# One fixed order for the first loads of an attention-plus-MLP kernel, with V as fp32 through SP's queue

## The chip, the cores and the metric

The kernel runs on one core of a Trainium2 chip. The metric is device time in microseconds (us), the median of the fast executions. A profile's span, from the first to the last instruction of the profiled execution, is about 2 us shorter than the time.

Engines in the profile: PE is the matmul engine (PEld its weight load), DVE the vector engine, ACT the scalar engine, POOL the engine called gpsimd in code, SP the engine that issues most loads. "SPq" is SP issuing.

## The reference

Eight batches, eight heads, 576 positions, head size 64. A sliding-window attention with a linear bias is followed by a normalised MLP with a residual:

```
scores = where(0 <= i - j < 128, q @ k.T / 8 - slope[h] * (i - j), -1e9)
x      = softmax(scores) @ v                    # -> (8, 576, 512)
xn     = (x - mean(x)) / sqrt(var(x) + 1e-6) * g
out    = x + relu(xn @ w1) @ w2                 # w1 512 x 2048, w2 2048 x 512
```

All inputs are fp32. The kernel computes in fp16 with fp32 accumulation.

## The kernel before

Attention works on head pairs: four per batch, `hp` 0 to 3. Each needs a q, a k and a V tile. The MLP works on chunks of 512 rows, nine in all, and is interleaved with the attention of the next batch. Batch 0's attention has no MLP to hide behind, and the first MLP chunk needs the first 512 of batch 0's 576 rows and all of w1. So everything up to the first MLP matmul is a head in which PE is mostly idle.

```python
def load_qk(b, hp):                      # fp32, issued by SP: six DMAs per head pair
    i = (b * HPAIRS + hp) % NSTG
    for src, dst in ((q, q32[i]), (k, k32[i])):
        ...
def load_v_all(b):                       # converted to fp16 on the way, issued by POOL
    ...
load_qk(0, 0)
nc.sync.dma_start(out=iden, ...)         # needed by every transpose
nc.sync.dma_start(out=mband, ...)        # masks, 512 KB
load_qk(0, 1)
nc.sync.dma_start(out=g_sb, ...)
load_v_all(0)
# ... cut: the mask copies on POOL, then
load_qk(0, 2)
load_qk(0, 3)
load_weights()                           # POOL: w1 in 4 column quarters, then w2 in 4
load_v_all(1)
scale_w1()                               # DVE: w1 *= g, 16 pieces of 128x512
drive(attn_gen(0), None, 0.0)
for c in range(NCHUNK):
    drive(attn_gen(c + 1) if c + 1 < B else None, mlp_gen(c), 1.0)
```

In `attn_gen` each head pair casts q and k to fp16 (DVE), transposes them on PE, copies the transposes out (`dst`), makes scores (`sc`), exponentials (ACT) and mask multiplies (`probs`, DVE), and multiplies by V (`ppv`). When a batch is done, DVE normalises it (`xs`), PE transposes it (`pxt`) and ACT copies it out (`xt`). `pm` is an MLP matmul. A scheduler decides the order on each engine ahead of time. At run time each engine works in that order, as the traces show it: in the changed kernel a statistics step of DVE (`mv`) had its input at 44.5 us and ran at 55.3, behind a cast for whose load DVE stood 10.2 us.

The softmax here doesn't subtract the row's maximum and nothing guards it: scores larger than these inputs give would overflow.

Of the kernel before, what the change touches and what calls it, by code (L numbers as in the profile page):

```python
# [10 lines left out]
FP32 = mybir.dt.float32  # L11
# [5 lines left out]
def kernel(  # L17
# [64 lines left out]
    NSTG = 4  # L82
    q32 = [persist.tile([P, NSB, 2, D], FP32, tag=f"q32{i}", name=f"q32_{i}") for i in range(NSTG)]
    k32 = [persist.tile([P, NSB, 2, D], FP32, tag=f"k32{i}", name=f"k32_{i}") for i in range(NSTG)]
    for t in q32 + k32:
        nc.vector.memset(t[TAIL:P, NSB - 1, :, :], 0.0)

    def load_qk(b, hp):
        i = (b * HPAIRS + hp) % NSTG
        for src, dst in ((q, q32[i]), (k, k32[i])):  # L90
            s = src[b, 2 * hp : 2 * hp + 2, :, :]
            for g in range(2):
                nc.sync.dma_start(  # L93
                    out=dst[:, 0:NFULL, g, :],
                    in_=s[g, 0 : NFULL * P, :].rearrange("(sb p) d -> p sb d", p=P),
                )
            nc.sync.dma_start(  # L97
                out=dst[0:TAIL, NFULL, :, :],
                in_=s[:, NFULL * P : S, :].rearrange("h p d -> p h d"),
            )  # L100

    vext = [persist.tile([P, NSB, H, VD], FP16, tag=f"vx{i}", name=f"vx_{i}") for i in range(2)]

    def load_v(b, hp):
        dst = vext[b % 2]
        s = v[b, 2 * hp : 2 * hp + 2, :, :]
        for sb in range(NSB):
            pb = P if sb < NFULL else TAIL
            nc.gpsimd.dma_start(
                out=dst[0:pb, sb, 2 * hp : 2 * hp + 2, 0:D],  # L110
                in_=s[:, sb * P : sb * P + pb, :].rearrange("h p d -> p h d"),
            )

    def load_v_all(b):
        dst = vext[b % 2]
        for sb in range(NSB):
            pb = P if sb < NFULL else TAIL
            nc.gpsimd.dma_start(  # L118
                out=dst[0:pb, sb, :, 0:D],
                in_=v[b, :, sb * P : sb * P + pb, :].rearrange("h p d -> p h d"),  # L120
            )

    nc.scalar.preload_act_table_set("natural_log_exp_and_others")
    eps_t = consts.tile([P, 1], FP32)
    nc.vector.memset(eps_t, eps)
    load_qk(0, 0)
    iden = consts.tile([P, P], FP16)
    nc.sync.dma_start(out=iden, in_=iden_dram.ap())
    mband = consts.tile([P, H, 2 * P], FP16)
    nc.sync.dma_start(out=mband, in_=m_dram.ap())  # L130
    load_qk(0, 1)
    g_sb = consts.tile([P, NKB], FP32)
    nc.sync.dma_start(out=g_sb, in_=moe_g_ln.rearrange("(kb p) -> p kb", p=P))
    for t in vext:
        nc.vector.memset(t[:, :, :, D:VD], 1.0)
        nc.vector.memset(t[TAIL:P, NSB - 1, :, :], 0.0)
    load_v_all(0)
    m2g = consts.tile([P, H, 512], FP16)
    nc.gpsimd.tensor_copy(m2g[:, :, 0:192], mband[:, :, 0:192])
    nc.gpsimd.tensor_copy(m2g[:, :, 192:256], mband[:, :, 0:64])  # L140
    nc.gpsimd.tensor_copy(m2g[:, :, 256:512], mband[:, :, :])
    xs_tail = [persist.tile([P, d_model], FP16, tag=f"xst{i}", name=f"xst_{i}") for i in range(2)]
    for t in xs_tail:
        nc.vector.memset(t[TAIL:P, :], 0.0)
# [3 lines left out]
    w1r = moe_w_ch1.rearrange("(kb p) f -> p kb f", p=P)  # L148
    w2r = moe_w_ch2.rearrange("(fb p) d -> p fb d", p=P)

    def load_weights():
        for f0 in range(0, ffn, 512):
            nc.gpsimd.dma_start(out=w1sb[:, :, f0 : f0 + 512], in_=w1r[:, :, f0 : f0 + 512])
        for f0 in range(0, NFB, 4):
            nc.gpsimd.dma_start(out=w2sb[:, f0 : f0 + 4, :], in_=w2r[:, f0 : f0 + 4, :])

    def scale_w1():
        for f0 in range(0, ffn, 512):
            for kb in range(NKB):
                nc.vector.tensor_scalar(  # L160
                    out=w1sb[:, kb, f0 : f0 + 512],
                    in0=w1sb[:, kb, f0 : f0 + 512],
                    scalar1=g_sb[:, kb : kb + 1],
                    scalar2=None,
                    op0=ALU.mult,
                )
# [10 lines left out]
    def attn_gen(b):  # L177
# [7 lines left out]
        for hp in range(HPAIRS):  # L185
            i = (b * HPAIRS + hp) % NSTG
            tr = []
            for stg, nm in ((q32[i], "q"), (k32[i], "k")):
                s16 = st16_pool.tile([P, NSB, P], FP16, tag=f"{nm}16")
                nc.vector.tensor_copy(  # L190
                    out=s16[:, :, :], in_=stg[:, :, :, :].rearrange("p s h d -> p s (h d)")
                )
                ptr = att_psum.tile([P, NSB * P], FP16, tag="att")
                for sb in range(NSB):
                    nc.tensor.transpose(  # L195
                        ptr[:, sb * P : sb * P + P], s16[:, sb, :], iden[:, :]
                    )
                dst = qt_pool.tile([P, NSB * P], FP16, tag=f"{nm}t")
                nc.vector.tensor_copy(out=dst[:, :], in_=ptr[:, :])  # L199
                tr.append(dst)  # L200
                yield
            nxt = b * HPAIRS + hp + NSTG
            if nxt < B * HPAIRS:
                load_qk(nxt // HPAIRS, nxt % HPAIRS)
            qt, kt = tr
            pr = []
            for grp in range(2):
                sc = sc_psum.tile([P, 2, 512], FP32, tag="sc")
                for j in ORDER[grp]:
                    for g in range(2):  # L210
                        r0 = D * g
                        nc.tensor.matmul(  # L212
                            sc[:, g, OFF[j] : OFF[j] + NQ[j]],
                            kt[r0 : r0 + D, j * P : j * P + P],
                            qt[r0 : r0 + D, j * P : j * P + NQ[j]],
                            start=True,
                            stop=True,
                        )
                probs = probs_pool.tile([P, 2, 512], FP16, tag=f"pr{grp}")
                nc.scalar.activation(  # L220
                    out=probs[:, :, :], in_=sc[:, :, :], func=AF.Exp, scale=inv_sqrt_d
                )
                if grp == 0:
                    view = probs[:, :, :].rearrange("p g (t c) -> p g t c", t=2)
                    nc.vector.tensor_tensor(  # L225
                        out=view,
                        in0=view,
                        in1=mband[:, 2 * hp : 2 * hp + 2, :]
                        .unsqueeze(2)
                        .broadcast_to([P, 2, 2, 2 * P]),  # L230
                        op=ALU.mult,
                    )
                else:
                    nc.vector.tensor_tensor(  # L234
                        out=probs[:, :, :],
                        in0=probs[:, :, :],
                        in1=m2g[:, 2 * hp : 2 * hp + 2, :],
                        op=ALU.mult,
                    )
                pr.append(probs)  # L240
                yield
            for g in range(2):
                h = 2 * hp + g
                ppv = att_psum.tile([P, NSB, D + 1], FP32, tag="att")
                for qb in range(NSB):
                    nc.tensor.matmul(  # L246
                        ppv[:, qb, :],
                        pr[GRP[qb]][:, g, OFF[qb] : OFF[qb] + P],
                        vx[:, qb, h, 0 : D + 1],
                        start=True,  # L250
                        stop=(qb == 0),
                    )
                    if qb > 0:
                        j = qb - 1
                        nc.tensor.matmul(  # L255
                            ppv[:, qb, :],
                            pr[GRP[j]][:, g, OFF[j] + P : OFF[j] + 2 * P],
                            vx[:, j, h, 0 : D + 1],
                            start=False,
                            stop=True,  # L260
                        )
                rec = small_pool.tile([P, NSB], FP32, tag="rec")
                nc.vector.reciprocal(out=rec[:, :], in_=ppv[:, :, D])  # L263
                nc.vector.tensor_tensor(
                    out=xb[:, 0:NSB, D * h : D * h + D],
                    in0=ppv[:, :, 0:D],
                    in1=rec[:, :].unsqueeze(2).broadcast_to([P, NSB, D]),
                    op=ALU.mult,
                )
                yield  # L270
        if b + 2 < B:
            load_v_all(b + 2)
        if b % 2 == 1:
            xp = xpair[b // 2]
            nc.sync.dma_start(
# [104 lines left out]
                if next(m_gen, StopIteration) is StopIteration:  # L380
                    m_gen = None

    load_qk(0, 2)
    load_qk(0, 3)
    load_weights()
    load_v_all(1)
    scale_w1()
    drive(attn_gen(0), None, 0.0)
    for c in range(NCHUNK):
        drive(attn_gen(c + 1) if c + 1 < B else None, mlp_gen(c), 1.0)  # L390

# [29 lines left out]
```

## Time and profile before

402.95 us (402.53 to 403.23 in three runs).

| stretch of the trace | length |
|---|---|
| start to first MLP matmul (head) | 75.8 us |
| first MLP matmul to the end | 324.8 us |
| start of MLP chunk 1 | 114.3 us |

Busy time by stretch of the kernel before: a window and its length in us, then the busy us (and count) of each engine, the granted clock, the share of DMA time and GB/s.

```profile
core 0: us, PE busy (x) PEld busy (x) DVE busy (x) ACT busy (x) POOL busy (x), PEclk, DMA share, GB/s
0.00:76.00 76.00, 18.59 (x178) 13.18 (x179) 32.08 (x93) 12.74 (x18) 22.70 (x30) 1.00 1.20 172
200.00:300.00 100.00, 99.26 (x787) 48.66 (x788) 70.81 (x169) 46.32 (x74) 8.40 (x10) 1.00 0.50 92
```

In the middle PE is 99% busy, so beyond the last 1% nothing is to be had there without less PE work. In the head PE works 19 of 76 us. The page's timeline, 40 slices of 10 us, shows what is busy there instead:

```profile
PE   0201153799999999999999999999999999999996
...
DMA  9999969932893393349444943791011003002002
```

The DMA engines are full for the first 40 us. The DMA view of those 40 us splits that by queue (packets, MB, share of engine time), and gives for each load the size of one issue and the median us from issue to landing:

```profile
q0 software_dynamic: 9866, 4.91, 89.2%
q1 hardware_dynamic: 8336, 2.41, 38.4%
...
k_1_105<-in_k_dram SPq DMA_DIRECT2D x2, 128.0 KB, 14.3
q_2_102<-in_q_dram SPq DMA_DIRECT2D x2, 128.0 KB, 16.6
k_2_106<-in_k_dram SPq DMA_DIRECT2D x2, 128.0 KB, 14.2
```

The software queue is POOL's: V of both batches and the weights. The hardware queue is SP's: q and k. An undisturbed q tile lands 2.5 us after its issue. Here it takes up to 16.6 us. The chain that ended last, in the first 80 us (start, length, what):

```profile
10.59 3.51 SPq L97
...
19.14 6.03 SPq L97
...
28.84 11.90 DMA k_2_106<-in_k_dram
...
42.95 6.38 DMA q_0_100<-in_q_dram
...
71.75 0.42 DVE xs L303
...
75.96 1.42 PE pm L335 x4
```

From 10 to 49 us the chain is loads almost alone. SP's issues take up to 6.0 us each, against 0.5 to 0.6 us undisturbed (the trace does not name what holds them). Then k of head pair 2 lands, then DVE, in its fixed order, stands before q of *batch 1*. The first transposes stood 10.5 us for the identity, which was issued behind six other loads.

### The profile page before, as it was taken

The page shows a single profiled execution, that of the slowest core. Times are in us where ns is not written, and L with a number is a line of the kernel's source. Part 1 is how long each engine was busy: PE and PEld are TensorE (multiplying, and loading weights), DVE is VectorE, ACT ScalarE, POOL GpSimd, SP SyncE. Part 2 cuts the span into 40 slices and gives each one's busy share as a digit, 9 for nine tenths or more (in the row PEclk, how much of TensorE's full clock was granted, in tenths as well). Part 3 has the DMA queues.
Part 4 walks back from the last instruction along what each step waited for, and adds up shares of the span by engine and source line. Part 5 has one row for each costly group of instructions (what it writes and reads, how often), then busy time and mean ns, then how long its engine had stood idle before and what let it go on. Part 6 is the DMA issues. An engine that isn't in the chain of part 4 may idle for free.

```text
span 400.6 us, 6433 instructions
## 1 busy us (share of the span) xinstructions
PE 337.4 (84%) x2528; PEld 167.5 (42%) x2528; DVE 227.2 (57%) x543; ACT 154.7 (39%) x249; POOL 43.7 (11%) x55
## 2 busy tenths in 40 slices
PE   0201153799999999999999999999999999999996
PEld 0100032455455445445444544454445445444442
DVE  3224366467857685767767766767785657222221
ACT  1200222563265436543562474266336543520510
POOL 6730004000400040004001200400000000000000
PEclk9999999999999999999999999999999999999999
DMA  9999969932893393349444943791011003002002
GB/s 149 200 197 186 175 143 157 130 85 61 144 193 68 81 170 91 74 103 179 113 105 98 137 98 82 124 191 30 0 54 55 0 28 111 28 5 75 26 26 81
DMA packets 125199, 40.58 MB, mean 101 GB/s; under 512 B 115824, under 2 KB 119920, under 8 KB 125168
## 3 DMA queue, kind: packets, MB, share of 16 engines
q1 hardware_dynamic: 83440, 31.25, 32.8%
q0 software_dynamic: 41728, 8.92, 24.8%
q8 instruction: 20, 0.33, 0.4%
q14 instruction: 11, 0.09, 0.1%
HBM read 37.26 MB, written 9.44 MB: 117 GB/s over the span
## 4 chain that ended last, share of the span: by engine, by line
PE 68%; ACT 12%; SPq 8%; DMA 5%; DVE 5%; issue 1%; DVEq 0%
PE pm L353 29%; PE pm L335 24%; ACT probs L220 9%; PE ptr L195 4%; SPq L93 4%; PE sc L212 4%; SPq L97 3%; PE pxt L313 3%; DMA k_2_106<-in_k_dram 3%; ACT ht L343 3%; PE ppv L246 3%; DVE probs L234 3%; PE ppv L255 2%; DMA q_0_100<-in_q_dram 2%; DVE st L287 1%
## 5 line engine op out<-in xcount | busy, mean ns | idle before, releaser
L353 PE MATMUL pm<-w2sb,ht 128*128 128x512 f16 x576 | 138.6, 379 | 0.0
L220 ACT ACTIVATE probs<-sc 128x1024 f16<-128x1024 f32 x64 | 65.4, 1022 | 97.4 <-PE sc L212 97.4
L343 ACT ACTIVATE ht<-pm 128x512 f16<-128x512 f32 x108 | 64.6, 598 | 75.8 <-PE pm L335 75.8
L353 PEld LDWEIGHTS <-ht 128*128 128x128 f16 x576 | 51.5, 98 | 50.3 <-issue 1.5
L335 PEld LDWEIGHTS <-w1sb 128*128 128x128 f16 x576 | 48.9, 98 | 47.5 <-issue 5.0
L246 PEld LDWEIGHTS <-probs 128*128 128x128 f16 x320 | 25.5, 101 | 43.0 <-DVE probs L234 19.7
L345 DVE TENSOR_SCALAR ht<-pm 128x512 f16<-128x512 f32 x36 | 24.8, 688 | 29.7 <-PE pm L335 29.7
L225 DVE TENSOR_TENSOR probs<-probs,mband 128x1024 f16<-128x1024 f16 x32 | 22.1, 692 | 33.7 <-ACT probs L220 33.7
L212 PE MATMUL sc<-dst 64*128 64x256 f16 (+2 forms) x320 | 26.9, 264 | 15.4 <-DVE dst L199 9.7
L199 DVE COPY dst<-ptr 128x640 f16<-128x640 f16 x64 | 31.1, 488 | 8.6 <-PE ptr L195 8.5
L246 PE MATMUL ppv<-vx_116,probs 128*128 128x65 f16 x160 | 16.4, 206 | 20.1 <-DVE probs L234 11.0
L212 PEld LDWEIGHTS <-dst 64*128 64x128 f16 x320 | 12.2, 97 | 41.3 <-DVE dst L199 22.6
L234 DVE TENSOR_TENSOR probs<-probs,m2g 128x1024 f16<-128x1024 f16 x32 | 22.0, 687 | 13.1 <-ACT probs L220 13.1
L118 POOL DMA_DIRECT2D vx_117<-in_v_dram x20 | 16.9, 866 | 108.2 <-PE ppv L255 102.0
L118 POOL DMA_DIRECT2D vx_116<-in_v_dram x20 | 16.9, 865 | 104.0 <-PE ppv L255 103.2
L290 ACT ACTIVATE lv<-mv,eps_t 128x4 f32<-128x4 f32 (+1 forms) x16 | 4.6, 295 | 50.3 <-DVE mv L288 49.4
L255 PEld LDWEIGHTS <-probs 128*128 128x128 f16 x256 | 20.5, 102 | 0.0
L263 DVE RECIPROCAL rec<-ppv 128x5 f32<-128x5 f32 x64 | 12.0, 194 | 14.8 <-PE ppv L255 14.4
L363 DVE TENSOR_TENSOR o_tile<-pm,xp_3182 128x512 f32<-128x512 f32 x9 | 6.2, 691 | 24.2 <-PE pm L353 24.2
L313 PE MATMUL pxt<-iden,xs 128*128 128x128 f16 x128 | 12.5, 230 | 5.7 <-DVE xs L303 5.5
L335 PE MATMUL pm<-xt_514,w1sb 128*128 128x512 f16 x64 | 17.0, 390 | 0.0
L335 PE MATMUL pm<-xt_546,w1sb 128*128 128x512 f16 x64 | 16.4, 380 | 0.0
(279 smaller groups left out, 390.9 us busy)
## 6 DMA issues: line engine op xcount, KB each, us to landing
out_dram<-o_tile SPq DMA_DIRECT2D x36, 256.0 KB, 2.5
q_0_100<-in_q_dram SPq DMA_DIRECT2D x16, 128.0 KB, 2.6
vx_116<-in_v_dram POOLq DMA_DIRECT2D x16, 128.0 KB, 5.2
k_0_104<-in_k_dram SPq DMA_DIRECT2D x16, 128.0 KB, 2.7
q_1_101<-in_q_dram SPq DMA_DIRECT2D x16, 128.0 KB, 2.7
w1sb<-in_moe_w_ch_dram POOLq DMA_DIRECT2D x4, 512.0 KB, 12.3
k_1_105<-in_k_dram SPq DMA_DIRECT2D x16, 128.0 KB, 2.5
q_2_102<-in_q_dram SPq DMA_DIRECT2D x16, 128.0 KB, 2.8
```

The costliest lines, as they stand in the source:

```text
L118: nc.gpsimd.dma_start(out=dst[0:pb, sb, :, 0:D], in_=v[b, :, sb * P : sb * P + pb, :].rearrange("h p d -> p h d"),)
L199: nc.vector.tensor_copy(out=dst[:, :], in_=ptr[:, :])
L212: nc.tensor.matmul(sc[:, g, OFF[j] : OFF[j] + NQ[j]], kt[r0 : r0 + D, j * P : j * P + P], qt[r0 : r0 + D, j * P : j * P + NQ[j]], start=Tr ...
L220: nc.scalar.activation(out=probs[:, :, :], in_=sc[:, :, :], func=AF.Exp, scale=inv_sqrt_d)
L234: nc.vector.tensor_tensor(out=probs[:, :, :], in0=probs[:, :, :], in1=m2g[:, 2 * hp : 2 * hp + 2, :], op=ALU.mult,)
L246: nc.tensor.matmul(ppv[:, qb, :], pr[GRP[qb]][:, g, OFF[qb] : OFF[qb] + P], vx[:, qb, h, 0 : D + 1], start=True, stop=(qb == 0),)
L255: nc.tensor.matmul(ppv[:, qb, :], pr[GRP[j]][:, g, OFF[j] + P : OFF[j] + 2 * P], vx[:, j, h, 0 : D + 1], start=False, stop=True,)
L313: nc.tensor.transpose(pxt[:, kb, :], xs[:, kb * P : kb * P + P], iden[:, :])
L335: nc.tensor.matmul(pm[:, :], w1sb[:, kb, fb * P : fb * P + P], xt[:, kb, :], start=(kb == 0), stop=(kb == NKB - 1),)
L343: nc.scalar.activation(out=ht[:, fb, :], in_=pm[:, :], func=AF.Relu)
L345: nc.vector.tensor_scalar(out=ht[:, fb, :], in0=pm[:, :], scalar1=0.0, scalar2=None, op0=ALU.max)
L353: nc.tensor.matmul(pm[:, :], ht[:, fb, tb * P : tb * P + P], w2sb[:, fb, :], start=(fb == 0), stop=(fb == NFB - 1),)
```

## The change

Its intent: batch 0's inputs first, then the weights, then batch 1. The identity goes first. V is loaded as fp32 through SP's queue, one head pair at a time, and cast on chip. The weights wait for head pair 2 of batch 0 to land, and batch 1 waits for w2's second quarter (manual dependencies, "gates"). To make room, batch 0's q/k casts go from DVE to ACT, its V casts and the w1 scaling go to POOL, and the mask copies are made per head pair.

```diff
-    def load_qk(b, hp):
+    def load_qkv(b, hp, after=None):
         i = (b * HPAIRS + hp) % NSTG
-        for src, dst in ((q, q32[i]), (k, k32[i])):
+        for src, dst in ((q, q32[i]), (k, k32[i]), (v, v32[i])):
...
+                if after is not None:
+                    tc.add_manual_dep(last.ins, after.ins.name, SYNC, reason="load order")
...
-    load_qk(0, 0)
     iden = consts.tile([P, P], FP16)
     nc.sync.dma_start(out=iden, in_=iden_dram.ap())
+    load_qkv(0, 0)
...
+    load_qkv(0, 1)
+    gates = {"w1": load_qkv(0, 2)}
+    load_qkv(0, 3)
...
+    def load_w1():
         for f0 in range(0, ffn, 512):
-            nc.gpsimd.dma_start(out=w1sb[:, :, f0 : f0 + 512], ...)
+            d = nc.gpsimd.dma_start(out=w1sb[:, :, f0 : f0 + 512], ...)
+            tc.add_manual_dep(d.ins, gates["w1"].ins.name, SYNC, reason="load order")
+        gates["w2"] = d
+    def load_w2():
...
+            tc.add_manual_dep(d.ins, gates["w1"].ins.name, SYNC, reason="load order")
+            if f0 == 4:
+                gates["next"] = d
...
-                nc.vector.tensor_scalar(          # w1 scaling
+                nc.gpsimd.tensor_scalar(
...
-                nc.vector.tensor_copy(            # q/k casts
+                if b == 0:
+                    nc.scalar.activation(out=s16[:, :, :], in_=src, func=AF.Copy)
+                else:
+                    nc.vector.tensor_copy(out=s16[:, :, :], in_=src)
...
+            (nc.gpsimd if b == 0 else nc.vector).tensor_copy(
+                out=vx[:, :, 2 * hp : 2 * hp + 2, 0:D], in_=v32[i][:, :, :, :]
+            )
...
-    load_qk(0, 2)
-    load_qk(0, 3)
-    load_weights()
-    load_v_all(1)
-    scale_w1()
+    load_w1()
     drive(attn_gen(0), None, 0.0)
+    load_w2()
+    scale_w1()
+    for hp in range(HPAIRS):
+        load_qkv(1, hp, gates["next"])
```

More of the change, by code (lines that the diff above doesn't have):

```diff
@@ L84 @@
     k32 = [persist.tile([P, NSB, 2, D], FP32, tag=f"k32{i}", name=f"k32_{i}") for i in range(NSTG)]
-    for t in q32 + k32:
+    v32 = [persist.tile([P, NSB, 2, D], FP32, tag=f"v32{i}", name=f"v32_{i}") for i in range(NSTG)]
+    for t in q32 + k32 + v32:
         nc.vector.memset(t[TAIL:P, NSB - 1, :, :], 0.0)
-    def load_qk(b, hp):
+    SYNC = mybir.DependencyInfo(mybir.DependencyClass.Sync, mybir.DependencyReason.DATA)
+    def load_qkv(b, hp, after=None):
         i = (b * HPAIRS + hp) % NSTG
-        for src, dst in ((q, q32[i]), (k, k32[i])):
+        last = None
+        for src, dst in ((q, q32[i]), (k, k32[i]), (v, v32[i])):
             s = src[b, 2 * hp : 2 * hp + 2, :, :]
             for g in range(2):
-                nc.sync.dma_start(
+                last = nc.sync.dma_start(
                     out=dst[:, 0:NFULL, g, :],
@@ L96, in load_qk @@
                 )
-            nc.sync.dma_start(
+                if after is not None:
+                    tc.add_manual_dep(last.ins, after.ins.name, SYNC, reason="load order")
+            tail = nc.sync.dma_start(
                 out=dst[0:TAIL, NFULL, :, :],
@@ L100, in load_qk @@
             )
+            if after is not None:
+                tc.add_manual_dep(tail.ins, after.ins.name, SYNC, reason="load order")
+        return last
     vext = [persist.tile([P, NSB, H, VD], FP16, tag=f"vx{i}", name=f"vx_{i}") for i in range(2)]
-    def load_v(b, hp):
-        dst = vext[b % 2]
-        s = v[b, 2 * hp : 2 * hp + 2, :, :]
-        for sb in range(NSB):
-            pb = P if sb < NFULL else TAIL
-            nc.gpsimd.dma_start(
-                out=dst[0:pb, sb, 2 * hp : 2 * hp + 2, 0:D],
-                in_=s[:, sb * P : sb * P + pb, :].rearrange("h p d -> p h d"),
-            )
-    def load_v_all(b):
-        dst = vext[b % 2]
-        for sb in range(NSB):
-            pb = P if sb < NFULL else TAIL
-            nc.gpsimd.dma_start(
-                out=dst[0:pb, sb, :, 0:D],
-                in_=v[b, :, sb * P : sb * P + pb, :].rearrange("h p d -> p h d"),
-            )
     nc.scalar.preload_act_table_set("natural_log_exp_and_others")
@@ L125, with mask_pair @@
     nc.vector.memset(eps_t, eps)
-    load_qk(0, 0)
     iden = consts.tile([P, P], FP16)
     nc.sync.dma_start(out=iden, in_=iden_dram.ap())
+    load_qkv(0, 0)
     mband = consts.tile([P, H, 2 * P], FP16)
     nc.sync.dma_start(out=mband, in_=m_dram.ap())
-    load_qk(0, 1)
     g_sb = consts.tile([P, NKB], FP32)
     nc.sync.dma_start(out=g_sb, in_=moe_g_ln.rearrange("(kb p) -> p kb", p=P))
+    load_qkv(0, 1)
+    gates = {"w1": load_qkv(0, 2)}
+    load_qkv(0, 3)
     for t in vext:
         nc.vector.memset(t[:, :, :, D:VD], 1.0)
-        nc.vector.memset(t[TAIL:P, NSB - 1, :, :], 0.0)
-    load_v_all(0)
+        nc.vector.memset(t[TAIL:P, NSB - 1, :, D:VD], 0.0)
     m2g = consts.tile([P, H, 512], FP16)
-    nc.gpsimd.tensor_copy(m2g[:, :, 0:192], mband[:, :, 0:192])
-    nc.gpsimd.tensor_copy(m2g[:, :, 192:256], mband[:, :, 0:64])
-    nc.gpsimd.tensor_copy(m2g[:, :, 256:512], mband[:, :, :])
+    def mask_pair(hp):
+        hs = slice(2 * hp, 2 * hp + 2)
+        nc.gpsimd.tensor_copy(m2g[:, hs, 0:192], mband[:, hs, 0:192])
+        nc.gpsimd.tensor_copy(m2g[:, hs, 192:256], mband[:, hs, 0:64])
+        nc.gpsimd.tensor_copy(m2g[:, hs, 256:512], mband[:, hs, :])
     xs_tail = [persist.tile([P, d_model], FP16, tag=f"xst{i}", name=f"xst_{i}") for i in range(2)]
@@ L149 @@
     w2r = moe_w_ch2.rearrange("(fb p) d -> p fb d", p=P)
-    def load_weights():
+    def load_w1():
         for f0 in range(0, ffn, 512):
-            nc.gpsimd.dma_start(out=w1sb[:, :, f0 : f0 + 512], in_=w1r[:, :, f0 : f0 + 512])
+            d = nc.gpsimd.dma_start(out=w1sb[:, :, f0 : f0 + 512], in_=w1r[:, :, f0 : f0 + 512])
+            tc.add_manual_dep(d.ins, gates["w1"].ins.name, SYNC, reason="load order")
+        gates["w2"] = d
+    def load_w2():
         for f0 in range(0, NFB, 4):
-            nc.gpsimd.dma_start(out=w2sb[:, f0 : f0 + 4, :], in_=w2r[:, f0 : f0 + 4, :])
+            d = nc.gpsimd.dma_start(out=w2sb[:, f0 : f0 + 4, :], in_=w2r[:, f0 : f0 + 4, :])
+            tc.add_manual_dep(d.ins, gates["w1"].ins.name, SYNC, reason="load order")
+            if f0 == 4:
+                gates["next"] = d
     def scale_w1():
@@ L189, in attn_gen @@
                 s16 = st16_pool.tile([P, NSB, P], FP16, tag=f"{nm}16")
-                nc.vector.tensor_copy(
-                    out=s16[:, :, :], in_=stg[:, :, :, :].rearrange("p s h d -> p s (h d)")
-                )
+                src = stg[:, :, :, :].rearrange("p s h d -> p s (h d)")
+                if b == 0:
+                    nc.scalar.activation(out=s16[:, :, :], in_=src, func=AF.Copy)
+                else:
+                    nc.vector.tensor_copy(out=s16[:, :, :], in_=src)
                 ptr = att_psum.tile([P, NSB * P], FP16, tag="att")
@@ L201, in attn_gen @@
                 yield
+            (nc.gpsimd if b == 0 else nc.vector).tensor_copy(
+                out=vx[:, :, 2 * hp : 2 * hp + 2, 0:D], in_=v32[i][:, :, :, :]
+            )
             nxt = b * HPAIRS + hp + NSTG
-            if nxt < B * HPAIRS:
-                load_qk(nxt // HPAIRS, nxt % HPAIRS)
+            if HPAIRS + NSTG <= nxt < B * HPAIRS:
+                load_qkv(nxt // HPAIRS, nxt % HPAIRS)
+            if b == 0:
+                mask_pair(hp)
             qt, kt = tr
@@ L270, in attn_gen @@
                 yield
-        if b + 2 < B:
-            load_v_all(b + 2)
         if b % 2 == 1:
@@ L381, in drive @@
                     m_gen = None
-    load_qk(0, 2)
-    load_qk(0, 3)
-    load_weights()
-    load_v_all(1)
+    load_w1()
+    drive(attn_gen(0), None, 0.0)
+    load_w2()
     scale_w1()
-    drive(attn_gen(0), None, 0.0)
+    for hp in range(HPAIRS):
+        load_qkv(1, hp, gates["next"])
     for c in range(NCHUNK):
```

## The prediction

> **What bounds the kernel now.** By stretches the span is two stages. After 76 us PE is about 99% busy (99.26 of 100 us in 200-300); before, nearly idle (19 us busy). The timeline shows the first MLP matmul at 75.8 us. In that head the chain of waits is SP issuing loads and DMA landings (SPq 26%, k_2 11%, q_0 6% of its first 110 us). The DMA engines are over 90% busy for 0-40 us: the gpsimd queue's V and weights take 89% of engine time and SP's q/k crawl (issue to landing 10-17 us against 2.5 later). V of batch 1 and both weights go ahead of head pairs 2 and 3; attention of batch 0 ends at 67.7 us.
>
> **What the change does.** V goes over SP: nine DMAs per head pair. Where SP is unhindered (52-62 us) three issues take 1.84 us, so a head pair costs 5.5 us of issue and lands 2.5 us later. Identity first saves the first transpose's 10.5 us wait. DVE gains 28 V casts of 0.49 us in batches 1-7 (14 us; DVE is at 71%: off the path). Batch 0's q/k casts go to ACT (about 0.7 us each, estimate from 1.02 us for 1024 columns), the w1 scaling to POOL (16 at about 0.6 us; its 128x512 copy took 0.61).
>
> **The new head, estimated from these durations.** Head pairs 0-2 and masks land by about 21.5 us; w1 is released then. POOL's order is: issue w1 (4 x 0.79 us), cast v2, cast v3, only then issue w2. Head pair 3's k and v share engines with w1 ([...]SP's q/k got about 37 GB/s beside the weights). v3 lands near 34 us, w2 issues at 35-38, its second quarter lands near 43-44 and releases batch 1. DVE's order places the casts of batch 1's first q and k *before* batch 0's normalisation (xs), so xs waits for k of batch 1, about 50 us; xs to the first MLP matmul took 4.0 us before. So the MLP starts near 54.5 us instead of 75.8: 21 us saved, all on the critical path.[...] Batch 1's head pairs come every 5.5 us and are used every 8.4; small stalls, 1-2 us. From there PE's 322 us are unchanged.
>
> **Prediction: 382 us, 375 to 393 eight times in ten.** Faster by over 2%: 0.93; within 2%: 0.06; slower: 0.01.
>
> **What would show it.** First MLP matmul at 52-58 us. Head pairs 0-2 landed by 22 us. w1's first issue at 21-22 us, w2's after the v3 cast, at 34-38. DVE's wait before the casts of batch 1's q/k ended by DMA near 48-50 us, xs straight after. No PE wait for POOL's w1 over 2 us. First MLP matmul to the end within 3 us of 322.
>
> **What would make it wrong.** Scaling on POOL slower than 1 us each[...]: PE then waits quarter after quarter (390 or more). Head pair 3 starved longer by w1, which delays w2 and batch 1 alike. Batch 1's loads too slow for DVE's in-order casts, so stalls spread past 60 us. Or w1 moves faster than 150 GB/s written, and all is 4-6 us earlier.

The sum: k of batch 1 at 50 us, 4.5 us from there to the first MLP matmul (54.5), 21 us less than before, so 402.95 - 21 = 382. The 37 GB/s can be read from the trace of before: from 14 to 24 us SP's queue moved 1602 packets and 0.37 MB, POOL's 1601 and 1.59 MB.

## The result

389.57 us (388.9 to 390.68, four runs) against 402.74 us (the three runs above and a fourth). The ratio is 0.9674 with a 95% interval of 0.9649 to 0.970. The kernel got 13.2 us faster. The prediction was 382 us (375 to 393), a gain of 21 us.

| | before | after | predicted |
|---|---|---|---|
| first MLP matmul | 75.8 us | 61.7 us | 54.5 us |
| from there to the end of the span | 324.8 us | 326.9 us | 322 us and 1 to 2 us of stalls |
| start of MLP chunk 1 | 114.3 us | 101.1 us | - |
| span | 400.6 us | 388.6 us | - |

The same windows and timeline rows of the changed kernel:

```profile
0.00:62.00 62.00, 18.97 (x178) 12.84 (x179) 26.41 (x71) 18.68 (x26) 35.10 (x41) 1.00 0.86 163
200.00:300.00 100.00, 99.31 (x786) 48.59 (x785) 75.17 (x176) 46.88 (x77) 0.00 (x0) 1.00 0.36 94
```

```profile
PE   2443109999999999999999999999999999999996
...
DMA  5799897667774676777657634630010004002002
```

The middle is as full of PE work as it was; DVE does 4 us more per 100 us there, the V casts, at no visible cost. The head is 14.1 us shorter. PE now works in its first 40 us (the row starts 2443) and is then almost idle for two slices. Batch 0's attention ends at 41.2 us instead of 67.7. The chain that ended last shows why:

```profile
23.50 0.55 SPq L97
24.10 14.03 DMA v_3_111<-in_v_dram
...
38.27 0.72 POOL vx_124 L206
38.99 0.68 POOL w2sb L154
39.67 8.35 DMA w2sb<-in_moe_w_ch_dram
48.09 0.37 SPq L97
...
50.91 5.08 DMA k_0_104<-in_k_dram
56.11 0.17 DVE s_596 L196
...
56.81 0.82 DVE xs L310 x2
...
61.92 1.71 PE pm L342 x4
```

Read it downwards. V of head pair 3 takes 14 us to land. POOL stands before its cast, and only behind that cast in POOL's order comes the issue of w2. The second quarter of w2 lands at 48.0 us and releases batch 1. Batch 1's first k lands at 56.0, DVE casts it, and only then comes xs, which the MLP needs. Each link was in the prediction. The times were not.

Issue to landing in the first 60 us, by load:

```profile
v_2_110<-in_v_dram SPq DMA_DIRECT2D x2, 128.0 KB, 2.5
...
k_3_107<-in_k_dram SPq DMA_DIRECT2D x2, 128.0 KB, 7.1
v_3_111<-in_v_dram SPq DMA_DIRECT2D x2, 128.0 KB, 13.3
```

Head pairs 0 to 2 now land undisturbed, and w1's first issue is released at 20.6 us. Head pair 3 shares the engines with w1. In the window from 28 to 34 us the two queues moved (packets, MB):

```profile
q0 software_dynamic: 945, 0.94, 91.8%
q1 hardware_dynamic: 939, 0.23, 29.7%
```

They moved nearly the same number of packets, as in the trace of before (1601 and 1602 from 14 to 24 us). In this window a weight packet writes about 1,000 bytes, a packet of k or V 250, so SP's queue got 0.23 MB in 6 us, 38 GB/s of the 194 that both moved. How the engines choose between the queues is not shown, and the counts are not always equal (303 and 406 from 26 to 28 us). But here the queue with the smaller packets got the smaller share of the bytes.

### The profile page after: what moved, and what is told of

The parts are those of the page before. It is cut to its first block, busy times and chain, and to the rows that moved or that the text cites. A ratio compares the mean times of both kernels' runs of the same rounds, so it can differ in the third digit from the quotient of the medians.

```text
span 388.6 us, 6535 instructions
## 1 busy us (share of the span) xinstructions
PE 339.5 (87%) x2528; PEld 166.8 (43%) x2528; DVE 241.3 (62%) x551; ACT 160.9 (41%) x257; POOL 40.5 (10%) x44
## 4 chain that ended last, share of the span: by engine, by line
PE 68%; ACT 11%; DMA 7%; SPq 6%; DVE 4%; issue 2%; POOL 0%; DVEq 0%; POOLq 0%
PE pm L360 29%; PE pm L342 24%; ACT probs L229 8%; PE ptr L199 4%; SPq L97 4%; DMA v_3_111<-in_v_dram 4%; PE sc L221 3%; PE pxt L320 3%; DVE probs L243 3%; PE ppv L255 3%; ACT ht L350 3%; DMA w2sb<-in_moe_w_ch_dram 2%; SPq L103 2%; PE ppv L264 2%; DMA k_0_104<-in_k_dram 1%
## 5 line engine op out<-in xcount | busy, mean ns | idle before, releaser
L352 DVE TENSOR_SCALAR ht<-pm 128x512 f16<-128x512 f32 x36 | 24.7, 687 | 27.4 <-PE pm L342 27.2
L320 PE MATMUL pxt<-iden,xs 128*128 128x128 f16 x128 | 12.9, 230 | 18.0 <-DVE xs L310 17.9
L162 POOL TENSOR_SCALAR w1sb<-w1sb,g_sb 128x512 f16<-128x512 f16 x16 | 25.4, 1609 | 0.1
L320 PEld LDWEIGHTS <-xs 128*128 128x128 f16 x128 | 9.0, 101 | 25.5 <-DVE xs L310 21.3
L342 PE MATMUL pm<-xt_488,w1sb 128*128 128x512 f16 x64 | 17.6, 403 | 0.0
L342 PE MATMUL pm<-xt_520,w1sb 128*128 128x512 f16 x64 | 16.6, 380 | 0.0
```

What stands on the lines that cost most here:

```text
L162: nc.gpsimd.tensor_scalar(out=w1sb[:, kb, f0 : f0 + 512], in0=w1sb[:, kb, f0 : f0 + 512], scalar1=g_sb[:, kb : kb + 1], scalar2=None, op0= ...
L320: nc.tensor.transpose(pxt[:, kb, :], xs[:, kb * P : kb * P + P], iden[:, :])
L342: nc.tensor.matmul(pm[:, :], w1sb[:, kb, fb * P : fb * P + P], xt[:, kb, :], start=(kb == 0), stop=(kb == NKB - 1),)
L352: nc.vector.tensor_scalar(out=ht[:, fb, :], in0=pm[:, :], scalar1=0.0, scalar2=None, op0=ALU.max)
```

## The experiments

Theory 1: the head is one chain of loads (SP's issues, V of head pair 3 beside w1, w2's issue, batch 1's release, k of batch 1, xs), and the gain is what that chain got shorter. The rivals, as the texts number them: the bytes that have to move set the start in any order, or batch 1's release alone does (both 1); the rate of w1's scaling on POOL binds (2); the order of the loads as such is most of the gain (3); V on SP's queue is what gains (4); the identity's place is what gains (5); batch 1 cannot be supplied any earlier, whatever the order (6). An edit also lets the scheduler choose a new order on DVE and POOL; where that bears on the reading it is said, because then two things differ. Every kernel below gave correct results. "First MLP" is the first MLP matmul, "chunk 1" the first matmul of MLP chunk 1.

| kernel | time, us | ratio to before (95%) | first MLP | chunk 1 | chunk 1 to end |
|---|---|---|---|---|---|
| before | 402.95 | 1 | 75.8 | 114.3 | 286.3 |
| the change | 389.57 | 0.9674 (0.9649-0.970) | 61.7 | 101.1 | 287.5 |
| w1_after_hp3 | 385.57 | 0.9577 (0.9547-0.9607) | 56.9 | 95.3 | 288.2 |
| b1_after_w1 | 392.62 | 0.9754 (0.9717-0.9792) | 63.5 | 103.0 | 287.7 |
| scale_on_dve | 391.21 | 0.9702 (0.9663-0.9741) | 62.2 | 102.1 | 287.3 |
| xs_first | 388.26 | 0.9629 (0.9595-0.9664) | 56.0 | 99.4 | 287.0 |
| no_gates | 397.66 | 0.9879 (0.9857-0.9902) | 69.8 | 109.6 | 286.3 |
| v_on_gpsimd | 383.93 | 0.9537 (0.9519-0.9555) | 50.1 | 95.4 | 286.3 |
| vcast_pool | 389.20 | 0.9664 (0.9637-0.9692) | 61.1 | 100.1 | 287.8 |
| mlp_first6 | 391.77 | 0.9733 (0.9705-0.9761) | 47.9 | 101.9 | 288.3 |
| before_iden_first | 402.57 | 0.9987 (0.996-1.0013) | 75.7 | 115.6 | 286.3 |
| iden_second | 389.69 | 0.9675 (0.9643-0.9707) | 60.4 | 99.6 | 288.0 |
| first6_in_turn | 391.62 | 0.9715 (0.969-0.974) | 47.3 | 94.5 | 294.3 |
| v_gpsimd_in_turn | 384.26 | 0.9544 (0.9525-0.9563) | 49.7 | 92.2 | 289.7 |

(The last column is the span less the column before it. Runs were made on several chips, so the ratios, not the medians, compare rows.)

### w1_after_hp3: does head pair 3 beside w1 cost what the chain says?

```diff
-    gates = {"w1": load_qkv(0, 2)}
-    load_qkv(0, 3)
+    load_qkv(0, 2)
+    gates = {"w1": load_qkv(0, 3)}
```

> w1 released one head pair later. Theory 1 (the head is one chain: v3 starved by w1, then the w2 issue behind the v3 cast, then w2's second quarter releasing batch 1): v3 lands at 27-29 us instead of 38.2, w2's first issue at about 30 us instead of 38.9, batch 1 released at about 45 us instead of 48.1, its first k landed near 53; also the scheduler now puts batch 0's xs ahead of batch 1's casts. First MLP matmul near 55 us instead of 61.7, time about 383 us (380-386). Rival 1 (the head is bound by the bytes that have to move before the MLP, in whatever order): first MLP matmul at 60-62 us, time 388-390. Rival 2 (w1's scaling on POOL bounds the MLP start): the scaling starts earlier, so the same gain as the start of the scaling, which would move from 42 to about 33 us: time about 380.

Measured: 385.57 us. w1 is issued later (27.3 us instead of 20.6) and yet w2 earlier (31.1 instead of 38.9), because V of head pair 3 no longer shares its way and lands at 27.2 instead of 38.1. That first link of theory 1 holds. The next gained little: w1's last quarter landed later (40.6 instead of 37.8), so 7.8 us of earlier issue brought w2's second quarter only 2.1 us forward (45.9) and batch 1's first k 1.9 us (54.1). In this stretch the bytes of the weights bind, as rival 1 says, though its number (388 to 390) failed. The first MLP matmul is at 56.9, but that is not w1's place alone: the scheduler now put batch 0's xs ahead of batch 1's casts (42.5 us instead of 56.8), and xs_first below, which changes only that, has its first MLP matmul at 56.0. Against xs_first this run is about 2 us faster (0.9577 and 0.9629 of before). The chain's last wait is now for batch 1 alone:

```profile
45.40 0.61 ACT xt L328
46.43 0.51 SPq L97
46.99 5.78 DMA q<-in_q_dram
52.85 0.50 DVE s L196
```

Batch 0 is normalised, transposed and copied by 46 us. PE then stands before the transposes of batch 1's first q, because its order has those ahead of the first MLP matmul.

### b1_after_w1: release batch 1 earlier

```diff
-        load_qkv(1, hp, gates["next"])
+        load_qkv(1, hp, gates["w2"])
```

The gate is now w1's last quarter instead of w2's second.

> Batch 1's loads released by w1's last quarter (about 37 us) instead of w2's second (48). Theory 1: released early they share the engines one packet for one with w2 from about 41 us on and crawl as head pair 3 did; and the order the scheduler gives puts casts of V of head pair 0 and of q of head pair 1 ahead of batch 0's xs, so xs waits for loads that land near 58-62 us. First MLP matmul at 62-67 us, time 389-394: no gain although the release is 11 us earlier. Rival 1 (release time of batch 1 alone sets the MLP start): about 10 us gained, first MLP matmul near 51, time about 379.

Measured: 392.62 us, slower than the change, as theory 1 expected. ("One packet for one" is head pair 3 beside w1 in the changed kernel, 939 packets and 945; in this run the packets were not counted.) Batch 1 was released near 38 us and its first k then took 12.2 us beside w2, instead of 5.1. So 10 us of earlier release became 2.7 us of earlier landing (53.3), and the release alone does not set the start. That the run even became slower is DVE's order: it now had V of head pair 0 and q of head pair 1 ahead of xs as well, which came at 59.4 us instead of 56.8.

### scale_on_dve: is POOL's scaling what binds?

```diff
-                nc.gpsimd.tensor_scalar(
+                nc.vector.tensor_scalar(
```

> w1 scaled on DVE again. Rival 2 (the scaling on POOL, 16 x 1.6 us from 42 to 67 us, holds the MLP up, by itself or by slowing DVE): scaling done by about 40 us, time 384 or less. Theory 1: nothing gained, since the MLP waits for xs and xs for batch 1's casts; in this build's order the cast of batch 1's q even stands before the statistics of batch 0, so xs comes about 3 us later (near 59.5), the ops after it run without POOL beside them (4.0 instead of 4.9 us): first MLP matmul near 63.5, time 390-392.

Measured: 391.21 us; the ratio's interval, 0.9663 to 0.9741, overlaps the change's. On POOL one piece takes 1.56 us and all sixteen run from 42.0 to 67.4 us. On DVE they take 0.35 us each and are done at 40 us. The end hardly cares, because PE uses w1 quarter by quarter and waited 0.28 us for POOL in all. That wait is what makes rival 2 fall; the time alone would not, since in this build's order xs came 1.5 us later (58.3). The run shows one more thing. The line of xs in the changed kernel, with POOL scaling at the same time, and in this one, with POOL idle (duration in ns, least/median/most):

```profile
L310 DVE TENSOR_SCALAR xs<-xp_186,mv,rstd x4: 402/761/770, 56.8 to 59.1; 128x512 f16<-128x512 f16 x4
```

```profile
L310 DVE TENSOR_SCALAR xs<-xp,mv,rstd x4: 396/400/400, 58.3 to 59.5; 128x512 f16<-128x512 f16 x4
```

Three of four take 0.76 us beside POOL's work; without it all take 0.40 us. So this step of DVE is slower while POOL scales. Two of these xs (57.49 to 58.26 and 58.18 to 58.58) began and ended inside one POOL instruction (57.41 to 59.05, and POOL's spans are rough), one of 0.77 us and one of 0.40. So by the trace DVE did not stand until that instruction was over; what sets the 0.36 us is not shown.

### xs_first: take the chain's last wait away

Batch 1's casts are made dependent on batch 0's last xs, so that DVE's order cannot put them ahead of it:

```diff
-                    nc.vector.tensor_copy(out=s16[:, :, :], in_=src)
+                    cst = nc.vector.tensor_copy(out=s16[:, :, :], in_=src)
+                    if b == 1:
+                        tc.add_manual_dep(cst.ins, last_xs[0].ins.name, SYNC, reason="after xs")
```

(and the same for the V cast)

> Only DVE's order is changed: batch 1's casts are made to wait for batch 0's last xs; loads and gates as in the change. Theory 1: xs at about 45 us instead of 56.8, then the first MLP matmul waits only for the transposes of batch 1's q (landed 54.8 plus cast 0.6 and transpose 0.7), which stand ahead of it in PE's order: about 56 us instead of 61.7, time about 384 (382-386). If DVE's order did not matter (the loads alone set the start): 388-390.

Measured: 388.26 us. The first MLP matmul came at 56.0 as expected, 5.7 us earlier, but chunk 1 began only 1.7 us earlier, and the time missed the expectation. Two windows show where the rest went:

```profile
60.00:64.00 4.00, 1.93 (x9) 0.62 (x9) 3.06 (x6) 1.55 (x3) 4.00 (x4) 0.85 0.67 152
64.00:68.00 4.00, 4.00 (x35) 1.94 (x35) 2.56 (x6) 2.17 (x3) 3.21 (x2) 0.72 0.65 146
```

PE stands (1.93 of 4 us busy) while DVE, in order, waits for q and k of batch 1's next head pairs. Then PE is busy but at a granted clock of 0.72, behind a gap of 2.2 us (59.9 to 62.1). In other runs below the clock fell behind gaps of 2.6 us (mlp_first6, 96.7 to 99.3 us; 0.50 in the window from 102 to 104), 3.6 us (first6_in_turn, 0.50), 4.0 us (v_on_gpsimd, 0.71) and 5.1 us (mlp_first6, 0.50). How long a gap it takes is not shown. And behind the 17.4 us that PE stood before batch 0's last transposes in the changed kernel the profile shows 1.00, although at its first MLP matmuls four took 1.71 us and later ones 0.86. The clock lost in the two windows is 0.15 x 4 + 0.28 x 4 = 1.7 us. Gap and clock make up 3.9 of the 4.0 us that the early start had lost again by chunk 1.

### no_gates: the same kernel without the order

```diff
-            tc.add_manual_dep(d.ins, gates["w1"].ins.name, SYNC, reason="load order")   # w1 and w2
-        load_qkv(1, hp, gates["next"])
+        load_qkv(1, hp)
```

> V on the SP ring, identity first, all as in the change, but no load waits for another: the weights start at about 1 us again, ahead of and beside everything. Theory 1 (the change's gates order the loads, but buy little of the gain, since both orders have the same bytes to move before batch 1's first tiles are in): w1 and w2 are in by about 28 us, batch 0's head pairs crawl till then and the last V lands near 45 us; batch 1's first tiles follow with no gate; the scheduler's order puts casts of batch 1's head pairs 1 and 2 ahead of batch 0's xs, so the first MLP matmul comes at about 61 us: time 386-394. Rival 3 (the order of loads is the gain): first MLP matmul after 70 us, time 397 or more.

Measured: 397.66 us. Theory 1's range was missed and rival 3's number held: without the gates only 1.2% of the 3.3% are left. The weights were issued from 1.2 us on and batch 0's tiles crept as before the change. V of head pair 3 landed near 45.6 us. The pieces of the chain:

```profile
42.06 3.55 DMA v<-in_v_dram
45.84 3.33 POOL w1sb L160 x2
50.71 7.54 POOL w1sb L160 x4
```

Here, unlike above, the slow scaling on POOL is on the chain. The scheduler put ten pieces of it ahead of the last V cast of batch 0, which ran at 58.2 us although its V had landed at 45.6, and PE stood 4.4 us for it. Batch 1's first k, for its part, landed 7.4 us earlier than with the gates (48.6). So taking the gates out cost about 0.02 x 403 = 8 of the 13 us, but up to 4.4 us of that may be POOL's order and not the order of the loads. A kernel without gates and with that cast first was not run. The other 5 us come from the rest of the change.

### v_on_gpsimd: V back on POOL's queue, the order kept

xs_first, but V is again loaded by POOL, converted on the way: batch 0 at the start, batch 1 behind w2's second quarter.

```diff
-        for src, dst in ((q, q32[i]), (k, k32[i]), (v, v32[i])):
+        for src, dst in ((q, q32[i]), (k, k32[i])):
...
+    load_v_all(0)
...
     load_w2()
+    load_v_all(1, gates["next"])
     scale_w1()
```

> The order of loads and xs first as in the run with xs first (388.3 us), but V goes over the gpsimd queue again, cast in flight, batch 0's at the start and batch 1's after w2. Theory 1 (V on the ring costs: 1.84 us of SP issue per tile of 288 KB, and v3 behind w1 holds back w2 and batch 1): without it w1 is released near 18 us, w2 follows w1 without a gap, batch 1's q and k are released near 37 us instead of 48 and come every 3.7 us, and the first MLP matmul comes at 47-50 us, now bound by batch 0's attention and POOL's scaling: time 374-382. Rival 4 (V on the fp32 ring is what gains, since the gpsimd queue's V starves SP): about as before the change, 395 or more.

Measured: 383.93 us, the fastest kernel: 0.9537 of before, against 0.9629 for xs_first. Rival 4 falls: V on SP's queue (with the casts on POOL and DVE that belong to it) is not the gain but costs about 4 us. SP's nine issues per head pair become six, w1 is released at 17.9 us instead of 20.6, and the first MLP matmul is at 50.1. The expected range, 374 to 382, was missed by 2 us. Windows of this run:

```profile
52.00:56.00 4.00, 2.29 (x10) 0.82 (x7) 1.88 (x3) 1.19 (x2) 4.00 (x4) 1.00 0.55 121
56.00:60.00 4.00, 1.71 (x7) 0.57 (x8) 2.26 (x5) 1.02 (x1) 4.00 (x3) 0.71 0.67 153
60.00:64.00 4.00, 4.00 (x34) 1.64 (x33) 2.46 (x4) 2.22 (x3) 4.00 (x4) 0.86 0.65 146
```

A PE wait of 4.0 us ends at 58.3 us (head pair 0's scores stand behind DVE's casts of head pairs that have not landed). Behind it the clock falls, to 0.71 and 0.86 in the last two windows.

### vcast_pool: are DVE's 28 V casts in the way?

```diff
-            (nc.gpsimd if b == 0 else nc.vector).tensor_copy(
+            (nc.gpsimd if b != 1 else nc.vector).tensor_copy(
```

> V casts of batches 2 to 7 on POOL (0.72 us each) instead of DVE (0.8). Theory 1: DVE's added casts are off the critical path once PE is full, so within 1.5 us of the change: 388-391, first MLP matmul to the end 325-328 us. If the 24 casts cost PE time, as much as 2 us less: first MLP matmul to the end about 325 and the time about 387.5.

Measured: 389.2 us, as expected. Off the path, though a V cast on DVE takes 0.8 us and not the 0.49 predicted.

### mlp_first6: start the MLP before batch 1

w1_after_hp3, with six MLP units ahead of batch 1's attention, and batch 1's casts each behind the mask multiply of the head pair before. During chunk 0 the MLP also gets 0.8 and not 1.0 units per step of attention, here and in first6_in_turn; what that does was not separated.

```diff
-        drive(attn_gen(c + 1) if c + 1 < B else None, mlp_gen(c), 1.0)
+        m_gen = mlp_gen(c)
+        for _ in range(6 if c == 0 else 0):
+            next(m_gen)
+        drive(attn_gen(c + 1) if c + 1 < B else None, m_gen, 0.8 if c == 0 else 1.0)
```

> w1 released after head pair 3 (385.6 us alone), and six MLP blocks of batch 0 are run before batch 1's attention starts, whose casts are made to wait for the fifth block and then for one another's head pair. Theory 1 (the MLP waits for batch 1's q only because its transposes stand ahead in PE's order; data of batch 0 and w1 are there at 46-47 us): first MLP matmul at 46.5-48.5 us instead of 56.9, then PE waits 2-4 us for batch 1's k (landing near 55) and for later head pairs; time 376-383. If w1's scaling on POOL (34 to 59 us) or the bytes still to come bound it after all, PE waits for them instead and the time stays at 384-387.

Measured: 391.77 us, a miss. The MLP started at 47.9 us as expected, and chunk 1 at 101.9, later than in w1_after_hp3 (95.3). At 73.5 to 79.5 us DVE stood 6.0 us for V of *batch 2*, which its order had placed ahead of batch 1's last head pair. My reading then was that DVE's order gave everything back.

### before_iden_first and iden_second: the identity's place

```diff
-    load_qk(0, 0)
     iden = consts.tile([P, P], FP16)
     nc.sync.dma_start(out=iden, in_=iden_dram.ap())
+    load_qk(0, 0)
```

(in the kernel before; in the changed kernel, the reverse)

> The kernel before, with nothing changed but the identity's load put first. Theory 1 (the head is bound by the order in which loads share the DMA engines; the rest of the change's gain is not in the identity): the 10.5 us wait of the first transposes goes, but batch 0's attention still ends when head pairs 2 and 3 have landed, near 67 us, and the first MLP matmul stays at 74-77 us: 400-404 us. Rival 5 (the 5 us that were gained without any gate come from having the identity first): 398.5 us or less, first MLP matmul at 72 us or less.

> The changed kernel with the identity's load behind head pair 0 instead of ahead of it, as it was before. Theory 1: the identity then lands near 9 us, some 6 us later than now, but the chain up to 38 us is SP's issues and v3's landing, which PE does not touch: 388.5-391.5 us, first MLP matmul at 61-63 us. Rival 5: 394 us or more.

Measured: 402.57 us (0.9987 of before) and 389.69 us (0.9675, against 0.9674 for the change). Both times are as theory 1 expected (the first MLP matmul of iden_second, 60.4 us, came 0.6 us before its range); rival 5 falls. The wait of 10.5 us before the first transposes vanished in the first run and nothing became faster, because the chain ran through k of head pair 2 (11.8 us of landing, from 28.6 to 40.4 us, as before).

### first6_in_turn: mlp_first6 with DVE's order mended

In mlp_first6 only batch 1's casts were held in turn. Here all from batch 1 on are:

```diff
-                    if b == 1:
-                        tc.add_manual_dep(cst.ins, (mult[hp - 1] if hp else evac[0, 4]).ins.name, SYNC, reason="in turn")
+            gate = None
+            if 1 <= b:
+                gate = mult[b, hp - 1, b > 1] if hp else mult[b - 1, HPAIRS - 1, 1] if b > 1 else evac[0, 4]
+                    if gate is not None:
+                        tc.add_manual_dep(cst.ins, gate.ins.name, SYNC, reason="in turn")
```

> As mlp_first6 (w1 behind head pair 3, six MLP units ahead of batch 1's attention), and besides every cast of q, k and V from batch 1 on must follow the mask multiply of the head pair before it, so that DVE's order holds no wait for a load that comes later than the work behind it. Theory 1 (what mlp_first6 gave back was DVE's order): first MLP matmul at 47-49 us, from there to the end 327-332 us instead of 342, so 376-382 us. Rival 6 (batch 1 and 2 simply cannot be supplied earlier, because w2 and the batches' loads fill the DMA engines up to about 70 us; an earlier start is always given back): from there to the end 338 us or more, 387 us or more.

Measured: 391.62 us, no better. My reading of mlp_first6 falls as the whole story, and the number of rival 6 held. The DVE wait is gone, but chunk 1 began at 94.5, no more than 0.8 us before w1_after_hp3, though the MLP had begun 9.6 us earlier. MLP chunk 0 was used up before batch 1 was normalised:

```profile
88.00:90.00 2.00, 0.00 (x0) 0.00 (x0) 1.76 (x6) 0.21 (x1) 0.00 (x0) 1.00 0.81 226
90.00:92.00 2.00, 0.41 (x5) 0.41 (x6) 1.53 (x5) 0.79 (x4) 0.00 (x0) 0.67 0.77 174
92.00:94.00 2.00, 1.70 (x14) 1.31 (x13) 0.91 (x3) 1.58 (x4) 0.00 (x0) 0.50 0.76 171
94.00:96.00 2.00, 1.85 (x12) 1.30 (x12) 0.00 (x0) 1.04 (x4) 0.00 (x0) 0.50 0.87 247
```

PE stood 3.6 us for batch 1's xs, and the clock was then 0.50 to 0.67 from 90 to 98 us, and 1.00 again from 98. (mlp_first6 shows the same behind its own gap of 5.1 us: 0.50 from 82 to 86 us.) And from chunk 1 to the end this kernel took 294.3 us, 6 more than any with free casts: holding every batch's casts in turn costs later on.

### v_gpsimd_in_turn: the fastest kernel without its wait of 4.0 us

```diff
-                    if b == 1:
-                        tc.add_manual_dep(cst.ins, last_xs[0].ins.name, SYNC, reason="after xs")
+                    if b > 0:
+                        gate = mult.get((b, hp - 1, int(b > 1)), mult.get((b - 1, HPAIRS - 1, 1)) if b > 1 else last_xs[0])
+                        tc.add_manual_dep(cst.ins, gate.ins.name, SYNC, reason="in turn")
```

> As v_on_gpsimd, but from batch 1 on each cast of q and k must follow the mask multiply of the head pair before it (the first of batch 1 still follows batch 0's last xs), so that head pair 0's scores no longer wait on DVE behind casts of head pairs that have not landed. In v_on_gpsimd that wait was one of 4.0 us at 58.3 us, and the granted clock fell to 0.71 and 0.86 of full speed in the 8 us around its end, although it was 1.00 before. Theory 1: first MLP matmul near 50 us,[...] no fall of the clock, from there to the end 327-329 us instead of 331.6, so 379-382 us. Rival 6 (the supply of batch 1 binds, whatever the order): waits of the same sum come back later, 383-386 us.

Measured: 384.26 us, the same as v_on_gpsimd (0.9544 and 0.9537). By the total rival 6 holds. By the trace theory 1's wait and clock came true and were paid for elsewhere (from the first MLP matmul to the end it took 332.2 us, not 327 to 329): the wait of 4.0 us is gone, the clock stays at 1.00 in all windows from 48 to 100 us, chunk 1 begins at 92.2 instead of 95.4. Then it loses 3.4 us chunk by chunk. The starts of MLP chunks 1 to 5 in the two traces are

```
v_on_gpsimd        95.4  133.4  171.2  209.2  246.9    (38.0, 37.8, 38.0, 37.7 apart)
v_gpsimd_in_turn   92.2  130.8  169.3  208.0  246.7    (38.6, 38.5, 38.7, 38.7 apart)
```

The constraint was needed for batch 1 and was put on all. A version that holds only batch 1's and batch 2's first casts, and might keep those 3 us, was not run; that it would is a guess.

## Why the prediction was right, and where it was off

The time fell inside the stated range, 7.6 us above its forecast, but of the marks set beforehand five were missed: the first MLP matmul (61.7 us, not 52 to 58), w1's first issue (20.6, not 21 to 22), w2's first issue (38.9, not 34 to 38), the landing that DVE waits for (56.0, not 48 to 50) and the stretch from the first MLP matmul to the end (326.9, not within 3 us of 322). The range was wide enough to cover them.

**Right: what binds.** The kernel is PE-bound behind the first MLP matmul and load-bound before it. All of the gain is in the head: chunk 1 begins 13.2 us earlier, and from there to the end the changed kernel takes 287.5 instead of 286.3 us.

**Right: the chain.** SP's issues, V of head pair 3, w2's issue behind POOL's cast, w2's second quarter, batch 1's first k, the cast, xs. w1_after_hp3 confirmed the first link (V of head pair 3 landed 11 us earlier) and xs_first the last (first MLP matmul at 56.0, though only 1.7 of these 5.7 us were left at chunk 1). The link in the middle, w2's issue to batch 1's release, turned out to hang on the bytes of the weights more than on the issue.

**Right: what is off the path.** DVE's V casts (vcast_pool), though their size was off (0.8 for 0.49 us).

**Mis-sized: "v3 lands near 34 us".** It landed at 38.1, and this is the largest term of the miss. The prediction had the rate right (37 GB/s; 38 measured) and shows no division by it. What was still to come when w1 was released was k and V of head pair 3, 2 x 288 KB or 0.59 MB. At 38 GB/s that is 15 us from k's first issue at 20.9, hence 36 at the earliest. From there the miss was carried, term by term:

| step | predicted | measured | added to the miss |
|---|---|---|---|
| V of head pair 3 landed | 34 | 38.1 | 4.1 |
| w2's second quarter landed | 43-44 | 48.0 | 0.4 |
| k of batch 1 landed | 50 | 56.0 | 1.5 |
| from there (cast, xs) to the first MLP matmul | 4.5 | 5.7 | 1.2 |
| first MLP matmul | 54.5 | 61.7 | 7.2 in all |

k of batch 1 shares the engines with w2's second half (from 50 to 53 us the weights moved 0.45 MB and SP's queue 0.20). The 5.7 us contain the slower xs beside POOL: from xs to the first MLP matmul it was 4.9 us instead of 4.0.

**Off, without consequence: POOL's scaling.** 1.56 us a piece and not 0.6, so the prediction's warning ("slower than 1 us each ... 390 or more") described the measured rate, but its consequence did not follow: PE waited 0.28 us. And no pause of POOL ahead of the scaling, on which the prediction had counted, is to be seen: POOL's last w2 issue ends at 41.9 and the first piece starts at 42.0.

**Off: "322 us are unchanged".** The trace of before has 324.8 from first MLP matmul to the end. With 2.1 us of new stalls the 326.9 measured are in line with what was expected of the stalls.

**Where the other gain is.** Taking out the gates costs about 8 of the 13 us (no_gates), of which up to 4.4 may be POOL's order in that build; none hang on the identity. V through SP's queue costs about 4 us rather than gaining. What the other 5 us consist of (ACT's casts of batch 0, DVE freed of the scaling, SP's order) was not separated and stays open.

**An order that was better.** Two small edits beat the change: w1 behind head pair 3, with the order on DVE that followed from it (385.6 us), and V back on POOL's queue with xs first (383.9 us).

## What to carry to other kernels

When two queues share the DMA engines, measure the rate that the small-packet queue gets (38 of 194 GB/s here, with packets of 250 bytes beside 1,000) and divide the bytes still to come by it, before deciding which load goes first. Here a large load held back until a small one had landed came 2.8 us later itself (w1, 40.6 for 37.8), the small one 11 us earlier (V, 27.2 for 38.1), and what waited for both 2.1 us earlier (w2, 45.9 for 48.0). After such an edit, look whether the scheduler changed another engine's order too, before crediting the edit. Measure an early start by when the *second* stage begins (chunk 1 here), since an earlier first stage is given back if the supply behind it has not moved. Constrain a scheduler's order only where a wait has been seen: a dependency that saved 3 us at the start cost 3 us spread over the batches after it.
